# Swapping the token halves of odd heads in a convolution by band matmuls, and making all bands by one product

## The chip, the cores and the metric

One NeuronCore of a Trainium2 chip. The metric is the device time of one execution in microseconds (us). A profile's span is some 1.7 to 2.1 us shorter than the time of the same execution, so times are compared with times and spans with spans. In this kernel TensorE does the matrix products, into tiles that the program places in banks of a memory called PSUM; VectorE, ScalarE and GpSimd do the element-wise work. The granted clock is the share of full speed at which TensorE was allowed to run.

## The reference

`x` is (8, 4096, 192): batch, tokens, channels; 8 heads of 24 channels. Each head has 7 taps, made positive by a softmax. A causal convolution over tokens is followed by a two-layer block with h cos(h) in between.

```python
w = exp(weight - max) / (sum + 1e-9)                    # per head, 7 taps
out[b, s, head] = sum_k w[head, k] * x_pad[b, s + k, head]   # 6 zero tokens ahead
h = out.reshape(32768, 192) @ w_in                      # d_ff = 2048
g = h * cos(h)
result = g @ w_out                                      # 32768 x 192, fp32
```

## The kernel before

Tokens are worked on in units of 1024 (eight blocks of 128 tokens, one token per partition) and in steps of 512 tokens, 64 steps in all. A block is convolved by a matmul with a band matrix, which has the 7 taps of a head along its diagonal. It is cut in two row halves of 64 partitions (tokens), which are seen at work at the same time (the timeline in the prediction shows a matmul of each starting at 109.66 us). The program keeps them on different PSUM banks. Only the last 6 tokens of the block before matter, and these lie in the lower half. So a head needs three matmuls of 64 rows by 192 columns: upper half, lower half, lower half of the block before (`prev`).

```python
    E, KP = 32 + K - 1, 8
    mask = consts.tile([128, E, KP], BF16)          # 1 where a tap lies on the diagonal
    ...
    prod = consts.tile([128, H, E, KP], BF16)
    for hs in (slice(0, 4), slice(4, 8)):           # mask times taps, then a sum over taps
        nc.vector.tensor_tensor(out=prod[:, hs], in0=mask..., in1=wn[:, hs]..., op=ALU.mult)
        for m in (4, 2):
            nc.vector.tensor_tensor(out=prod[:, hs, :, 0:m], in0=prod[:, hs, :, 0:m], in1=prod[:, hs, :, m : 2 * m], op=ALU.add)
        for q in range(4):
            p = slice(32 * q, 32 * q + 32)
            nc.vector.tensor_tensor(out=band[p, hs, 32 * q : 32 * q + E], in0=prod[p, hs, :, 0], in1=prod[p, hs, :, 1], op=ALU.add)
    ...
    def cast_unit(u, n0=0, n1=UB):                  # fp32 tokens to bf16, on GpSimd
        copy = nc.scalar.copy if u == 0 and n0 == 0 else nc.gpsimd.tensor_copy
        ...
        copy(out=bf[u][:, n0 + 1 : n1 + 1, :].rearrange("p n (h k r) -> p (n h) k r", h=H, k=NC),
             in_=x_tiles[u][:, n0:n1, :].rearrange("p n (h r k) -> p (n h) k r", h=H, k=NC))
    ...
    def conv_part(u, c, n0=0, n1=UB):               # four heads, two halves at a time
        ps = h_pool.tile([128, 2, T], FP32, name="h")
        ...
        mm(0, up, start=True)                       # heads 0, 1: bank 0; heads 2, 3: bank 1
        mm(2, lo, start=True)
        m = mm(1, up)
        mm(2, lo, 1)                                # 1: the block before
        mm(3, lo)
        turn = Turn()                               # keeps the halves on different banks
        turn.mark(m, mm(3, lo, 1))
        yield
        turn.wait(mm(0, lo))
        mm(0, lo, 1)
        mm(1, lo)
        turn.wait(mm(2, up))
        mm(1, lo, 1, stop=True)
        mm(3, up, stop=True)
        yield
        ...                                         # ScalarE takes the result out of PSUM
```

The order of work in a step is written down: `h0` to `h7` are the eight tiles of h (6 matmuls of 64 rows by 512 columns each), `c1` and `c2` the first and the second six of the twelve matmuls of a conv part (four heads of a unit; there is one such part in a step), `m8` stands for 8 pairs (upper, lower) of the second layer's matmuls (o_ps, 64 rows by 192 columns). The h tiles and the conv share three PSUM buffers. ScalarE makes the cosine (`s`), VectorE multiplies it with h, and that frees the buffer. In `ACT_ORDER`, `P` and `Q` take results of o_ps out of PSUM, and `ec` those of the conv.

```python
    h_pool = ctx.enter_context(tc.tile_pool(name="h_ps", bufs=3, space=PSUM))
    PE_ORDER = "h0 c1 m8 c2 h1 m8 h2 h3 m16 | h4 h5 m8 h6 m12 h7 m12"
    ACT_ORDER = "P s0 ec s1 s2 s3 Q s4 s5 s6 s7"
```

Of the kernel before, what the change touches and what calls it, by code (L numbers as in the profile page):

```python
# [9 lines left out]
BF16 = mybir.dt.bfloat16  # L10
AF = mybir.ActivationFunctionType
ALU = mybir.AluOpType
# [4 lines left out]
def kernel(  # L17
# [8 lines left out]
    nc = tc.nc  # L26
    B, S, D = x.shape
    H, K = weight.shape
# [13 lines left out]
    NC = D // 64  # L42
    R = G // NC
# [3 lines left out]
    consts = ctx.enter_context(tc.tile_pool(name="consts", bufs=1))  # L47
# [16 lines left out]
    x_tiles = {}  # L64
# [13 lines left out]
    for q in range(2):  # L78
        for t in range(2):
            nc.sync.dma_start(out=w_f[64 * t : 64 * t + 64, :, q * HP : (q + 1) * HP, :].rearrange("p k j f -> p k (j f)"),  # L80
                              in_=w_src[t, :, :, q * HP * 128 : (q + 1) * HP * 128])
# [11 lines left out]
    def keep_warm(n):  # L93
        for _ in range(n):
# [11 lines left out]
    xb0 = xbf_pool.tile([128, UB + 1, D], BF16, name="x_bf")  # L106
    nc.gpsimd.memset(xb0[:, 0, :], 0.0)

    E, KP = 32 + K - 1, 8
    mask = consts.tile([128, E, KP], BF16)  # L110
    nc.gpsimd.memset(mask[0:32], 0.0)
    nc.gpsimd.affine_select(out=mask[0:32], in_=mask[0:32], compare_op=ALU.not_equal, fill=1.0, base=1 - K,
                            pattern=[[1, E], [1, KP]], channel_multiplier=-1)
    for q in range(1, 4):
        nc.gpsimd.tensor_copy(out=mask[32 * q : 32 * q + 32], in_=mask[0:32])
    ident = consts.tile([128, 128], BF16)
    nc.gpsimd.memset(ident, 0.0)
    nc.gpsimd.affine_select(out=ident, in_=ident, compare_op=ALU.not_equal, fill=1.0, base=0, pattern=[[1, 128]],
                            channel_multiplier=-1)
    wn = consts.tile([128, H, 1, KP], BF16)  # L120
    nc.vector.memset(wn, 0.0)
    band = consts.tile([128, H, 256], BF16)
    nc.vector.memset(band, 0.0)

# [2 lines left out]
    wexp = consts.tile([128, H, K], FP32)  # L127
# [4 lines left out]
    nc.vector.tensor_reduce(out=wsum[:, :, 0], in_=wexp, axis=mybir.AxisListType.X, op=ALU.add)  # L132
    winv = consts.tile([128, H, 1], FP32)
    nc.vector.reciprocal(winv, wsum)
    nc.vector.tensor_tensor(out=wn[:, :, 0, 0:K], in0=wexp, in1=winv.to_broadcast([128, H, K]), op=ALU.mult)


    prod = consts.tile([128, H, E, KP], BF16)
    for hs in (slice(0, 4), slice(4, 8)):
        nc.vector.tensor_tensor(out=prod[:, hs], in0=mask.rearrange("p (o e) k -> p o e k", o=1).to_broadcast([128, 4, E, KP]),  # L140
                                in1=wn[:, hs].to_broadcast([128, 4, E, KP]), op=ALU.mult)
        for m in (4, 2):
            nc.vector.tensor_tensor(out=prod[:, hs, :, 0:m], in0=prod[:, hs, :, 0:m], in1=prod[:, hs, :, m : 2 * m], op=ALU.add)  # L143
        for q in range(4):
            p = slice(32 * q, 32 * q + 32)
            nc.vector.tensor_tensor(out=band[p, hs, 32 * q : 32 * q + E], in0=prod[p, hs, :, 0], in1=prod[p, hs, :, 1], op=ALU.add)  # L146

    w = consts.tile([128, NC, NP, 128], BF16)
    wo = consts.tile([128, NP, 2, D], BF16)
# [18 lines left out]
    bf = {}  # L168

    def cast_unit(u, n0=0, n1=UB):  # L170
        copy = nc.scalar.copy if u == 0 and n0 == 0 else nc.gpsimd.tensor_copy
        if u == 0:
            bf[u] = xb0
        else:
            bf[u] = xbf_pool.tile([128, UB + 1, D], BF16, name="x_bf")
            if u % UPS == 0:
                nc.gpsimd.memset(bf[u][:, 0, :], 0.0)  # L177
            else:
                nc.gpsimd.tensor_copy(out=bf[u][:, 0, :], in_=bf[u - 1][:, UB, :])  # L179

        copy(out=bf[u][:, n0 + 1 : n1 + 1, :].rearrange("p n (h k r) -> p (n h) k r", h=H, k=NC),  # L181
             in_=x_tiles[u][:, n0:n1, :].rearrange("p n (h r k) -> p (n h) k r", h=H, k=NC))
        bf.pop(u - 2, None)

    ct_tiles = {}
# [1 line left out]
    def conv_view(ps, n):  # L187

        return ps[:, :, 0 : n * 2 * G].rearrange("p b (n k i r) -> p b i n k r", n=n, k=NC, i=2)

    def conv_mm(u, c, pv, i, rows, prev, n0, n1, **flags):
        h = 4 * c + i
        return nc.tensor.matmul(  # L193
            out=pv[:, i // 2, i % 2],
            lhsT=band[rows, h, 128 if prev else 0 : 256 if prev else 128],
            rhs=bf[u][rows, n0 + 1 - prev : n1 + 1 - prev, h * G : (h + 1) * G].rearrange("p n (k r) -> p n k r", k=NC),
            skip_group_check=True, **flags)

    def conv_out(u, c, ps, n0, n1, copies, double=False):
        for b in range(2):  # L200
            w0 = (2 * c + b) * 2 * R
            o = ct_tiles[u][:, n0:n1, :, :, w0 : w0 + 2 * R].rearrange("p n k t w -> p (n k) t w")
            i = ps[:, b, 0 : (n1 - n0) * 2 * G].rearrange("p (m t w) -> p m t w", t=1, w=2 * R)
            if double:
                copies[b](o, i.to_broadcast([128, (n1 - n0) * NC, 2, 2 * R]))  # L205
            else:
                copies[b](o[:, :, 0, :], i[:, :, 0, :])  # L207

    def conv_part(u, c, n0=0, n1=UB):


        ps = h_pool.tile([128, 2, T], FP32, name="h")
        pv = conv_view(ps, n1 - n0)
        up, lo = slice(0, 64), slice(64, 128)

        def mm(i, rows, prev=0, **flags):
            return conv_mm(u, c, pv, i, rows, prev, n0, n1, **{"start": False, "stop": False, **flags})

        mm(0, up, start=True)
        mm(2, lo, start=True)  # L220
        m = mm(1, up)
        mm(2, lo, 1)
        mm(3, lo)
        turn = Turn()
        turn.mark(m, mm(3, lo, 1))
        yield
        turn.wait(mm(0, lo))
        mm(0, lo, 1)
        mm(1, lo)
        turn.wait(mm(2, up))  # L230
        mm(1, lo, 1, stop=True)
        mm(3, up, stop=True)
        yield
        if c == 0 and u not in ct_tiles:
            ct_tiles[u] = ct_pool.tile([128, UB, NC, 2, 64], BF16, name="ct")
        conv_out(u, c, ps, n0, n1, [nc.scalar.copy] * 2)
        yield
# [14 lines left out]


    cast_unit(0, 0, NB)
    cast_unit(0, NB, UB)
    ct_tiles[0] = ct_pool.tile([128, UB, NC, 2, 64], BF16, name="ct")
    cT[0] = cT_pool.tile([128, UB, NC, 128], BF16, name="cT")
    copies = [nc.scalar.copy, nc.vector.tensor_copy]
# [35 lines left out]
    for q in range(2):  # L294
        for i in range(2):
            nc.sync.dma_start(out=wo_f[:, q * HP : (q + 1) * HP, i], in_=wo_src[:, q * HP : (q + 1) * HP, i])
    nc.gpsimd.tensor_copy(out=w[:, :, HP:NP], in_=w_f[:, :, HP:NP])
    cast_unit(1)
    for q in range(2):
        nc.gpsimd.tensor_copy(out=wo[:, q * HP : (q + 1) * HP], in_=wo_f[:, q * HP : (q + 1) * HP])  # L300
# [67 lines left out]
    for t in range(NT + 2):  # L368
        u, second = divmod(t, TPU)
        cu, cc = (u + 2, 0) if second else (u + 1, 1)  # L370
        conv = {"c": conv_part(cu, cc) if cu < NU else iter(())}
        if t == 0:
            conv["d"] = conv_part(1, 0)
        act, done, h, step = (ACT_ORDER if t > 1 else ACT_FIRST[t]).split(), set(), {}, 0
# [72 lines left out]
```

## Time and profile before

| | before |
|---|---|
| time, median | 745.55 us |
| span of the profile | 744.1 us |
| TensorE, VectorE, ScalarE, GpSimd busy | 98%, 83%, 84%, 18% |
| one step of 512 tokens in the steady part | 11.120 us |

The prediction below shows the lines of the page and of the timelines. In a timeline the columns are: start, busy time, engine, line of the kernel, operation, what it writes and reads, shapes, count, and in brackets the idle time ahead of it with what ended it. A matmul's bar (0.24 us with 192 columns) is longer than the time between two starts of one half (0.082 us), so bars overlap, and starts are what is read here.

### The profile page before, as it was taken

How to read it: one execution, taken by the hardware profiler on the slowest of the kernel's cores; microseconds unless marked ns; L12 is line 12 of the kernel's file. 1: busy time of each engine (PE TensorE's matmuls, PEld its weight loads, DVE VectorE, ACT ScalarE, POOL GpSimd, SP SyncE). 2: the span in 40 equal slices, each digit the busy share in tenths (PEclk: the TensorE clock that was granted, in tenths of full speed). 3: DMA queues.
4: the chain of work that ended last, by engine and by line, in shares of the span. 5: the costliest groups of instructions: out<-in, count | busy, mean ns of one | idle time of the engine just before them, and what ended most of it. 6: DMA issues, size and time to landing. Idle time of an engine off the chain costs nothing.

```text
span 744.1 us, 26716 instructions
## 1 busy us (share of the span) xinstructions
PE 727.9 (98%) x12073; PEld 647.4 (87%) x12073; DVE 619.7 (83%) x541; ACT 624.2 (84%) x776; POOL 134.2 (18%) x111
## 2 busy tenths in 40 slices
PE   5899999999999999999999999999999999999997
PEld 3489999999999999999999999999999999999876
DVE  7788888888888888888888888888888888888893
ACT  3788888888888888888888888888888888888883
POOL 4522102222102222201222201222201222201000
PEclk9999999999999999999999999999999999999999
DMA  7753354354355454354354255354245454243302
GB/s 171 181 118 95 100 129 104 92 130 100 95 129 110 86 129 104 91 129 120 75 129 111 87 127 126 73 126 119 83 122 129 78 119 124 81 118 86 87 23 65
DMA packets 167939, 79.96 MB, mean 107 GB/s; under 512 B 99474, under 2 KB 167058, under 8 KB 167826
## 3 DMA queue, kind: packets, MB, share of 16 engines
q1 hardware_dynamic: 167824, 78.26, 42.9%
q8 instruction: 94, 1.54, 0.9%
q14 instruction: 19, 0.16, 0.1%
q10 hardware_dynamic: 2, 0.00, 0.0%
HBM read 28.31 MB, written 25.17 MB: 72 GB/s over the span
## 4 chain that ended last, share of the span: by engine, by line
PE 96%; DVE 3%; ACT 1%; issue 0%; DVEq 0%
PE h L315 47%; PE o_ps L341 45%; PE h L193 3%; DVE g L325 1%; DVE band L146 0%; DVE prod L143 0%; ACT cs L321 0%; DVE prod L140 0%; ACT ct L207 0%; PE o_ps L95 0%; ACT o_sb L353 0%; DVE w L291 0%; PE h L274 0%; PE o_ps L102 0%; DVE zero L90 0%
## 5 line engine op out<-in xcount | busy, mean ns | idle before, releaser
L325 DVE TENSOR_TENSOR g<-h,cs 128x1024 bf16<-128x1024 f32 x512 | 605.3, 1221 | 107.4 <-ACT cs L321 100.5
L321 ACT ACTIVATE cs<-h 128x1024 bf16<-128x1024 f32 x512 | 511.5, 1025 | 75.0 <-PE h L315 70.2
L341 PE MATMUL o_ps<-wo,g 64*128 64x192 bf16 x8192 | 451.4, 243 | 1.2 <-ACT o_sb L353 1.2
L341 PEld LDWEIGHTS <-g 64*128 64x128 bf16 x8192 | 419.2, 94 | 35.5 <-SPq L159 1.8
L315 PE MATMUL h<-cT,w 64*128 64x512 bf16 x3072 | 436.4, 377 | 4.3 <-DVE g L325 2.0
L315 PEld LDWEIGHTS <-w 64*128 64x128 bf16 x3072 | 233.1, 94 | 40.3 <-issue 6.0
L243 POOL COPY ct<-ct 128x1536 bf16<-128x1536 bf16 (+1 forms) x32 | 46.4, 1449 | 548.0 <-ACT ct L207 542.5
L193 PE MATMUL h<-x_bf,band 64*128 64x192 bf16 (+1 forms) x776 | 73.0, 244 | 5.1 <-DVE band L146 4.7
L181 POOL CAST x_bf<-x_f 128x1536 bf16<-128x1536 f32 (+1 forms) x32 | 72.4, 2262 | 2.1 <-DMA x_f<-in_x_dram 2.1
L207 ACT CAST ct<-h 128x384 bf16<-128x384 f32 (+1 forms) x126 | 54.0, 480 | 21.3 <-PE h L193 21.3
L353 ACT COPY o_sb<-o_ps 128x384 f32<-128x384 f32 x128 | 61.3, 479 | 10.1 <-PE o_ps L341 8.2
L193 PEld LDWEIGHTS <-band 64*128 64x128 bf16 (+1 forms) x776 | 55.3, 95 | 11.2 <-DVE band L146 5.3
L179 POOL COPY x_bf<-x_bf 128x192 bf16<-128x192 bf16 x24 | 8.6, 358 | 0.0
L95 PE MATMUL o_ps<-zero 128*128 128x512 bf16 x19 | 6.3, 493 | 1.3 <-DVE zero L90 1.3
L205 ACT CAST ct<-h 128x384 bf16<-128x384 f32 x2 | 1.0, 480 | 6.9 <-PE h L193 6.9
L95 PEld LDWEIGHTS <-zero 128*128 128x128 bf16 x19 | 2.0, 116 | 4.3 <-issue 1.9
L300 POOL CAST wo<-wo_f 128x1536 bf16<-128x1536 f32 x2 | 2.9, 1469 | 4.2 <-DMA wo_f<-in_moe_w_out_dram 4.2
L146 DVE TENSOR_TENSOR band<-prod 32x152 bf16<-32x152 bf16 x8 | 3.3, 417 | 0.1
L143 DVE TENSOR_TENSOR prod<-prod 128x608 bf16<-128x608 bf16 (+1 forms) x4 | 3.0, 760 | 0.1
L98 ACT ACT_TABLE_LOAD x1 | 1.3, 1283 | 1.3 <-PEq L431 1.3
L205 DVE CAST ct<-h 128x384 bf16<-128x384 f32 x2 | 1.1, 558 | 0.9 <-ACT ct L205 0.8
L177 POOL MEMSET x_bf<- 128x192 bf16 x7 | 1.8, 258 | 0.0
(36 smaller groups left out, 20.9 us busy)
## 6 DMA issues: line engine op xcount, KB each, us to landing
out_dram<-o_sb SPq DMA_DIRECT2D x64, 384.0 KB, 3.0
x_f<-in_x_dram SPq DMA_DIRECT2D x31, 768.0 KB, 5.6
w_f<-in_moe_w_in_dram SPq DMA_DIRECT2D x4, 384.0 KB, 7.8
wo_f<-in_moe_w_out_dram SPq DMA_DIRECT2D x4, 384.0 KB, 5.0
x_f<-in_x_dram SPq DMA_DIRECT2D x2, 384.0 KB, 4.3
cT<-ct SPq DMA_TRANSPOSE x32, 5.6
w_row<-in_weight_dram ACTq DMA_DIRECT2D x1, 0.2 KB
```

Of the source, the lines that this page charges most:

```text
L95: nc.tensor.matmul(out=idle, lhsT=zero[:, 0:128], rhs=zero, start=True, stop=True)
L146: nc.vector.tensor_tensor(out=band[p, hs, 32 * q : 32 * q + E], in0=prod[p, hs, :, 0], in1=prod[p, hs, :, 1], op=ALU.add)
L179: nc.gpsimd.tensor_copy(out=bf[u][:, 0, :], in_=bf[u - 1][:, UB, :])
L181: copy(out=bf[u][:, n0 + 1 : n1 + 1, :].rearrange("p n (h k r) -> p (n h) k r", h=H, k=NC), in_=x_tiles[u][:, n0:n1, :].rearrange("p n (h ...
L193: return nc.tensor.matmul(out=pv[:, i // 2, i % 2], lhsT=band[rows, h, 128 if prev else 0 : 256 if prev else 128], rhs=bf[u][rows, n0 + 1 ...
L207: copies[b](o[:, :, 0, :], i[:, :, 0, :])
L243: nc.gpsimd.tensor_copy(out=ct[:, n0:n1, :, 1, :], in_=ct[:, n0:n1, :, 0, :])
L315: nc.tensor.matmul(out=h[:, i, :], lhsT=w[rows, k, j, :], rhs=c[rows, n0 : n0 + NB, k, :], start=(k == 0), stop=(k == NC - 1))
L321: nc.scalar.activation(out=cs, in_=h, func=AF.Sin, bias=math.pi / 2.0, scale=1.0)
L325: nc.vector.tensor_tensor(out=g_tiles[t][:, 2 * j : 2 * j + 2, :], in0=h, in1=cs, op=ALU.mult)
L341: m = nc.tensor.matmul(out=o_ps[tt, b][:, si * D : (si + 1) * D], lhsT=g_tiles[tt][rows, f, s * 128 : (s + 1) * 128], rhs=wo[rows, f // 2, ...
L353: nc.scalar.copy(o_sb[t][:, 2 * b : 2 * b + 2, :].rearrange("p s d -> p (s d)"), o_ps.pop((t, b))[:, 0 : 2 * D])
```

## The change

The intent: give both row halves the same work. If the tokens of the odd heads are stored with the two halves of each block exchanged, the odd heads' last 6 tokens lie in the upper half, and so does their third matmul. Four heads then need 6 and 6 matmuls in place of 4 and 8. The cast becomes three copies (even heads; odd heads down; odd heads up). The bands are made by one product over all heads, four sums, and eight copies dealt to VectorE, ScalarE and GpSimd.

```diff
-    prod = consts.tile([128, H, E, KP], BF16)
-    ... (mask times taps and sums by groups of four heads, as above)
+    prod = consts.tile([128, K, H, E], BF16)
+    nc.vector.tensor_tensor(out=prod, in0=mask.rearrange("p k (o e) -> p k o e", o=1).to_broadcast([128, K, H, E]),
+                            in1=wn.rearrange("p h (k o) -> p k h o", o=1).to_broadcast([128, K, H, E]), op=ALU.mult)
+    for d, n, m in ((0, 3, 3), (0, 1, 1), (2, 1, 4), (0, 1, 2)):
+        nc.vector.tensor_tensor(out=prod[:, d : d + n], in0=prod[:, d : d + n], in1=prod[:, d + m : d + m + n], op=ALU.add)
+    copies = [nc.vector.tensor_copy, nc.scalar.copy, nc.gpsimd.tensor_copy]
+    for odd in range(2):
         for q in range(4):
+            e0 = 32 * (q ^ (2 * odd))
+            copies[(4 * odd + q) % 3](out=band[32 * q : 32 * q + 32, odd:H:2, e0 : e0 + E],
+                                      in_=prod[32 * q : 32 * q + 32, 0, odd:H:2, :])
     ... (cut)
-        copy(out=bf[u][:, n0 + 1 : n1 + 1, :].rearrange("p n (h k r) -> p (n h) k r", h=H, k=NC),
-             in_=x_tiles[u][:, n0:n1, :].rearrange("p n (h r k) -> p (n h) k r", h=H, k=NC))
+        o = bf[u][:, n0 + 1 : n1 + 1, :].rearrange("p n (h t k r) -> t p (n h) k r", t=2, k=NC, r=R)
+        i = x_tiles[u][:, n0:n1, :].rearrange("p n (h t r k) -> t p (n h) k r", t=2, k=NC, r=R)
+        copy(out=o[0], in_=i[0])
+        copy(out=o[1, 0:64], in_=i[1, 64:128])
+        copy(out=o[1, 64:128], in_=i[1, 0:64])
     ... (cut)
+        mm(0, 0, start=True)      # head, half; 0 is the upper half
+        mm(2, 1, start=True)
+        mm(1, 0)
+        mm(2, 1, 1)
+        m = mm(1, 0, 1)
+        turn.mark(m, mm(3, 1))
         yield
+        m = mm(2, 0)
+        turn.wait(m, mm(0, 1))
+        mm(3, 0)
+        mm(0, 1, 1)
+        mm(3, 0, 1, stop=True)
+        mm(1, 1, stop=True)
```

More of the change, by code (lines that the diff above doesn't have):

```diff
@@ L107 @@
     nc.gpsimd.memset(xb0[:, 0, :], 0.0)
-    E, KP = 32 + K - 1, 8
-    mask = consts.tile([128, E, KP], BF16)
+    E = 32 + K - 1
+    mask = consts.tile([128, K, E], BF16)
     nc.gpsimd.memset(mask[0:32], 0.0)
     nc.gpsimd.affine_select(out=mask[0:32], in_=mask[0:32], compare_op=ALU.not_equal, fill=1.0, base=1 - K,
-                            pattern=[[1, E], [1, KP]], channel_multiplier=-1)
+                            pattern=[[1, K], [1, E]], channel_multiplier=-1)
     for q in range(1, 4):
@@ L119 @@
                             channel_multiplier=-1)
-    wn = consts.tile([128, H, 1, KP], BF16)
-    nc.vector.memset(wn, 0.0)
+    wn = consts.tile([128, H, K], BF16)
     band = consts.tile([128, H, 256], BF16)
@@ L134 @@
     nc.vector.reciprocal(winv, wsum)
-    nc.vector.tensor_tensor(out=wn[:, :, 0, 0:K], in0=wexp, in1=winv.to_broadcast([128, H, K]), op=ALU.mult)
-    prod = consts.tile([128, H, E, KP], BF16)
-    for hs in (slice(0, 4), slice(4, 8)):
-        nc.vector.tensor_tensor(out=prod[:, hs], in0=mask.rearrange("p (o e) k -> p o e k", o=1).to_broadcast([128, 4, E, KP]),
-                                in1=wn[:, hs].to_broadcast([128, 4, E, KP]), op=ALU.mult)
-        for m in (4, 2):
-            nc.vector.tensor_tensor(out=prod[:, hs, :, 0:m], in0=prod[:, hs, :, 0:m], in1=prod[:, hs, :, m : 2 * m], op=ALU.add)
+    nc.vector.tensor_tensor(out=wn, in0=wexp, in1=winv.to_broadcast([128, H, K]), op=ALU.mult)
+    prod = consts.tile([128, K, H, E], BF16)
[5 more added lines that the diff above has]
+    for odd in range(2):
         for q in range(4):
-            p = slice(32 * q, 32 * q + 32)
-            nc.vector.tensor_tensor(out=band[p, hs, 32 * q : 32 * q + E], in0=prod[p, hs, :, 0], in1=prod[p, hs, :, 1], op=ALU.add)
+            e0 = 32 * (q ^ (2 * odd))
+            copies[(4 * odd + q) % 3](out=band[32 * q : 32 * q + 32, odd:H:2, e0 : e0 + E],
+                                      in_=prod[32 * q : 32 * q + 32, 0, odd:H:2, :])
     w = consts.tile([128, NC, NP, 128], BF16)
@@ L213, in conv_part @@
         pv = conv_view(ps, n1 - n0)
-        up, lo = slice(0, 64), slice(64, 128)
+        sides = [slice(0, 64), slice(64, 128)]
         def mm(i, rows, prev=0, **flags):
-            return conv_mm(u, c, pv, i, rows, prev, n0, n1, **{"start": False, "stop": False, **flags})
-        mm(0, up, start=True)
-        mm(2, lo, start=True)
-        m = mm(1, up)
-        mm(2, lo, 1)
-        mm(3, lo)
+            return conv_mm(u, c, pv, i, sides[rows], prev, n0, n1, **{"start": False, "stop": False, **flags})
+        mm(0, 0, start=True)
[3 more added lines that the diff above has]
+        m = mm(1, 0, 1)
         turn = Turn()
-        turn.mark(m, mm(3, lo, 1))
+        turn.mark(m, mm(3, 1))
         yield
-        turn.wait(mm(0, lo))
-        mm(0, lo, 1)
-        mm(1, lo)
-        turn.wait(mm(2, up))
-        mm(1, lo, 1, stop=True)
-        mm(3, up, stop=True)
+        m = mm(2, 0)
[4 more added lines that the diff above has]
+        mm(1, 1, stop=True)
         yield
```

## The prediction

- The lower half's sums (11,119 and 10,954 ns) are made of the times between two starts of one half. The starts in the trace of the changed kernel give them: 82.5 ns with 192 columns (114 runs of 24 o_ps matmuls, 12 a half) and 215.8 ns with 512 (228 groups of six h matmuls, three a half), at a granted clock of 1.00. The kernel before shows that the halves run on independently: o_ps matmuls start at 109.66, 109.74 and 109.82 us, while conv matmuls that come ahead of them in the program start as late as 109.83 us. The trace does not name the half of a matmul, but the counts (of the first six conv matmuls, two above and four below) fit.
- The sum came to 5.6 us for the steady part and 1.3 us for the start, 6.9 us in all. The bands' product and sums both were to be done at about 9.0 us. The 9.9, 12.0 and 18.1 us follow from that 9.0, which was the author's estimate; no trace of the kernel before has the product's new form. For the sums alone, its trace gives an estimate of 1.7 us (a VectorE product of 1216 elements took 0.79 us and one of 56 took 0.22, so 912 elements would take 0.64 and 304 some 0.34).

> **What bounds the kernel now.** I read, in this order: the chain of waits, the costliest groups, the timeline of one steady stretch engine by engine, and the first 20 us.
>
> The chain and the three matmul groups of the page:
>
> ```profile
> PE 96%; DVE 3%; ACT 1%; issue 0%; DVEq 0%
> ...
> L341 PE MATMUL o_ps<-wo,g 64*128 64x192 bf16 x8192 | 451.4, 243 | 1.2 <-ACT o_sb L353 1.2
> L315 PE MATMUL h<-cT,w 64*128 64x512 bf16 x3072 | 436.4, 377 | 4.3 <-DVE g L325 2.0 <-ACT w L291 1.1 <-DVE w L291 0.8
> ...
> L193 PE MATMUL h<-x_bf,band 64*128 64x192 bf16 (+1 forms) x776 | 73.0, 244 | 5.1 <-DVE band L146 4.7
> ```
>
> TensorE is the bound, and nearly all matmuls use 64 rows: two row halves can work at once. So the question is which half. The chain in order of time gives the length of one step (one tile of 512 tokens); the same link comes back after 11.11 us (11.120 us on average from 45 to 689 us):
>
> ```profile
> 101.17 1.36 PE h L315 x12
> ...
> 112.28 1.36 PE h L315 x12
> ```
>
> The timeline of TensorE around the conv of such a step (start, length, group, count):
>
> ```profile
> 108.93 0.81 PE L315 MATMUL h<-cT,w 64*128 64x512 bf16 x5
> 109.49 0.33 PE L193 MATMUL h<-x_bf,band 64*128 64x192 bf16 x3
> 109.66 0.24 PE L341 MATMUL o_ps<-wo,g 64*128 64x192 bf16 x1
> 109.66 0.24 PE L193 MATMUL h<-x_bf,band 64*128 64x192 bf16 x1
> 109.74 0.24 PE L341 MATMUL o_ps<-wo,g 64*128 64x192 bf16 x1
> 109.74 0.24 PE L193 MATMUL h<-x_bf,band 64*128 64x192 bf16 x1
> ...
> 112.11 0.37 PE L315 MATMUL h<-cT,w 64*128 64x512 bf16 x1
> 112.12 0.24 PE L341 MATMUL o_ps<-wo,g 64*128 64x192 bf16 x1
> 112.21 1.46 PE L315 MATMUL h<-cT,w 64*128 64x512 bf16 x11
> ```
>
> At 109.66 the upper half has run out of conv work (2 matmuls) and starts on o_ps, while the lower half still does conv (4 matmuls). The halves are thus two queues that run on independently, each starting a 192-column matmul every 0.082 us. The lower one has more to do: per step 24 matmuls of h, 64 of o_ps and 8 of conv, against 24, 64 and 4 above.
>
> [...] for the lower half 24 x 215.8 + 72 x 82.5 = 11,119 ns, against the 11.120 us measured. So **the lower row half is busy all the time, and it is the bound**; the upper one idles 4 x 82.5 = 330 ns a step. [...] the same two additions took 1.89 us while a GpSimd cast ran (6.22 to 7.44) and 1.22 us later. [...]
>
> **The change, part by part.**
>
> Conv in the steady state. A head needs three matmuls: upper rows, lower rows, and lower rows of the block before. With the halves of odd heads swapped, their third one goes to the upper half. Per part of 4 heads: 6 and 6 in place of 4 and 8; the number of matmuls, 12, stays, and no weight load is added. The lower half then has 70 short matmuls: 24 x 215.8 + 70 x 82.5 = 10,954 ns, so 165 ns less. There are 62 parts; two fall in step 0, one in step 1, and 59 in full steps. Ceiling: 59 x 0.165 = 9.7 us.
>
> The wait behind it. h tiles live in three buffers; the third h of a step reuses the first one's. That path, from the timelines of ScalarE and VectorE:
>
> ```profile
> 109.78 1.02 ACT L321 ACTIVATE cs<-h 128x1024 bf16<-128x1024 f32 x1 [0.17 <-PE h L315]
> ...
> 110.83 1.23 DVE L325 TENSOR_TENSOR g<-h,cs 128x1024 bf16<-128x1024 f32 x1 [0.41 <-ACT cs L321]
> ```
>
> The first h ends at 109.74 (108.93 + 0.81), cosine to 110.80, product to 112.06, and the upper half starts the third h at 112.11. That start is already set by VectorE; the lower half comes at 112.21 and does not feel it. Between the first and the third h stand all 8 lower conv matmuls, so after the change the lower half would be there at 112.21 - 0.165 = 112.04, and the buffer comes free at 112.11 as before: both engines were idle ahead of those two instructions, so this path does not shrink. A **new wait of 0.07 us** a step; the saving is 0.165 - 0.07 = 0.095 us, and 59 x 0.095 = **5.6 us**. I looked for the next such wait: the sixth h waits for the third's product; as everything after the third h moves along with it, I find some 0.08 us of room there.
>
> Casts on GpSimd. A unit's cast (1536 elements, 2.30 us) becomes three of 768; one of 768 took 1.22 us on 128 partitions, and I take 64 partitions to cost the same. So 3.66 us, 31 times, in a step of 11 us in which GpSimd is otherwise idle after 4.1 us; the result is read a step later. It is hidden. Products of VectorE took 1.225 us beside GpSimd work and 1.221 without, so the longer overlap costs it nothing to speak of.
>
> The start. The bands of heads 4 to 7 come last:
>
> ```profile
> 5.03 0.79 DVE L140 TENSOR_TENSOR prod<-mask,wn 128x1216 bf16<-128x1216 bf16 x1
> 5.85 1.89 DVE L143 TENSOR_TENSOR prod<-prod 128x608 bf16<-128x608 bf16 x2
> 7.77 1.71 DVE L146 TENSOR_TENSOR band<-prod 32x152 bf16<-32x152 bf16 x4
> ...
> 11.60 1.70 DVE L146 TENSOR_TENSOR band<-prod 32x152 bf16<-32x152 bf16 x4
> ```
>
> and TensorE waits from 10.05 to 13.36 for them. [...] Eight copies are dealt to three engines, three on ScalarE at some 0.3 us each: 9.9. But ScalarE's cast of the first half unit, done by 6.83 before, now stands behind these copies, as three of 384 elements, which I put at 0.7 each (1.23 for 768): about 12.0. All 32 conv matmuls follow, in place of 24 after 13.36. The granted clock from 13.3 to 17.0 us was 0.63 on average; eight took 0.64 us there and 0.34 at full clock. The rest of the way to the steady h stream (15.34 to 18.85) stays at 3.5 us. So h starts at 12.0 + 2.6 + 3.5 = 18.1, or about 17 at full clock, against 18.85: 0.7 to 1.9 us earlier, I take **1.3 us**. Steps 0 and 1 are bound by ScalarE and VectorE, and pass it on.
>
> Sum: 5.6 + 1.3 = 6.9 us; 745.5 - 6.9 = **738.6 us**, 0.9% less.
>
> **Rivals.** (a) Nothing takes the lower half's place: the full 9.7 us, 734.5 us with the start. For it speaks that the lower half is full to within 1 ns; against it the third h, whose start is already VectorE's. (b) VectorE or ScalarE becomes the bound: they are busy 83% and 84%, and back to back their instructions start every 1.14 and 0.92 us, 8 x 1.14 = 9.1 us a step. As a rate neither binds; as a latency VectorE does, once a step. Should several h buffers do so, 0.05 us a step are left: 741 us. (c) The slack was hidden anyway, as the upper half runs ahead on o_ps: then no gain. Against it: running ahead helps the upper half alone; the lower starts without a gap. (d) The start gets worse, because the casts on ScalarE and GpSimd now queue behind the band copies: up to 2 us lost[...]; 741 us.
>
> **Range and chances.** The steady part is worth 0.06 to 0.165 us a step (3.5 to 9.7 us), the start -1 to +2.5 us. The extremes hardly meet, so 734.5 to 741.5 us holds it 8 times in 10. 2% faster would be 730.6 us, below even the ceiling: 3%. Slower by 2% would need the bound to move: 2%.
>
> **What would show it.** The step should be 11.02 us in the chain, with conv matmuls in pairs, 6 a half; 10.95 says (a), 11.12 says (c). Idle time of TensorE ahead of the third h, ended by VectorE's product, should be about 0.07 us a step, where there was none. GpSimd should be busy near 175 us. [...] the first conv matmul should come near 12 us and the h stream near 18 us. I am wrong if swapped partitions make the GpSimd casts several times slower, or if TensorE's clock falls at the start.

## The result, and the profile after

The changed kernel took 740.13 us (739.96 to 740.39, 4 runs) against 745.53 us (745.43 to 746.20, 4 runs). The ratio is 0.9926, with a 95% interval of 0.9909 to 0.9943. A ratio here is the mean time of one kernel's runs over the mean of the other's in the same rounds, so it isn't quite the ratio of the medians. The gain is 5.4 us, 0.7%; 6.9 us were predicted, and the time lies in the range. All changes in this document are under 2%, so they rest on such intervals and on the lengths of the steps.

Three stretches add up to the 5.84 us between the two spans (744.07 and 738.23). To measure them I took the start of VectorE's first product of steps 2 and 60.

| | before | after | gain |
|---|---|---|---|
| up to step 2 | 44.11 us | 43.02 us | 1.09 us |
| 58 steps, 2 to 60 | 644.96 us, 11.120 each | 640.41 us, 11.042 each | 4.55 us |
| after that | 55.00 us | 54.79 us | 0.20 us |

The first row is not a clean measure. Between 5 and 25 us the mean granted clock was 0.83 in the profile before and 0.91 in the one after. The first three experiments leave everything up to step 2 as it was, so their profiles show the same two starts again. At 0.83, step 2 came at 44.11 us (before) against 43.45 and 43.53 (experiments one and two); at 0.91, at 43.71 (experiment three) against 43.02 (after). So at a like clock the new start gains 0.6 to 0.7 us, as far as these five profiles go. With 59 steps of 0.078 us and 0.1 us at the end (0.20 without step 60, which is one of the 59) that makes 5.3 to 5.4 us, as the times have it.

TensorE's groups on the page of the changed kernel (busy us and mean ns; then the idle time ahead):

```profile
L347 PE MATMUL o_ps<-wo,g 64*128 64x192 bf16 x8192 | 409.0, 243 | 1.2 <-ACT o_sb L359 1.2
L321 PE MATMUL h<-cT,w 64*128 64x512 bf16 x3072 | 402.9, 377 | 4.1 <-DVE g L331 1.7
...
L198 PE MATMUL h<-x_bf,band 64*128 64x192 bf16 (+1 forms) x776 | 55.3, 241 | 4.1 <-ACT x_bf L185 1.7
```

The counts and the length of one matmul are as before, but the busy times fell by 42, 34 and 18 us against the lines in the prediction. That is no saving of 94 us: a group's busy time is the union of its bars, and now the halves run the same groups side by side, their starts 0.02 us apart, so bars of the same group lie over each other. The page can't tell what the change is worth. TensorE is still busy 98% of the span. The weight loads are counted in the same way: 12,073 of them, of 94 ns in the median, covered 87% of the span before and 75% after, though their lengths add up to 1,138 us in both.

The timeline of TensorE in the steady part of the changed kernel:

```profile
107.35 0.83 PE L321 MATMUL h<-cT,w 64*128 64x512 bf16 x6
107.99 0.43 PE L198 MATMUL h<-x_bf,band 64*128 64x192 bf16 x6
108.24 0.84 PE L347 MATMUL o_ps<-wo,g 64*128 64x192 bf16 x16
108.90 0.43 PE L198 MATMUL h<-x_bf,band 64*128 64x192 bf16 x6
109.15 0.83 PE L321 MATMUL h<-cT,w 64*128 64x512 bf16 x6
109.80 0.84 PE L347 MATMUL o_ps<-wo,g 64*128 64x192 bf16 x16
110.55 1.47 PE L321 MATMUL h<-cT,w 64*128 64x512 bf16 x12
```

The conv no longer mixes with o_ps; 6 conv matmuls take 0.25 us from start to start (107.99 to 108.24), three pairs of 0.0825. But the last link shows the new wait. Eight pairs of o_ps begin at 109.80, so the third h could begin at 109.80 + 8 x 0.0825 = 110.46. It begins at 110.55. VectorE's product of the first h, in the timeline of VectorE, ends at 109.27 + 1.23 = 110.50, just ahead of it:

```profile
109.27 1.23 DVE L331 TENSOR_TENSOR g<-h,cs 128x1024 bf16<-128x1024 f32 x1 [0.41 <-ACT cs L327]
```

The chain in order of time shows the same as a length. The third and fourth h together take 1.38 us, the fifth and sixth 1.29 us with the same 12 matmuls:

```profile
102.30 1.29 PE h L321 x12
...
110.64 1.38 PE h L321 x12
```

No view lists that wait as idle time. A matmul's bar lasts 0.24 us, and a hold-up of 0.09 us between starts disappears under it.

The start, in the timelines of VectorE, ScalarE and TensorE of the changed kernel:

```profile
5.02 2.38 DVE L137 TENSOR_TENSOR prod<-mask,wn 128x2128 bf16<-128x2128 bf16 x1
7.43 1.56 DVE L140 TENSOR_TENSOR prod<-prod 128x912 bf16<-128x912 bf16 x4
...
9.02 0.98 ACT L147 COPY band<-prod 32x152 bf16<-32x152 bf16 x3 [3.33 <-DVE prod L140]
10.03 0.70 ACT L185 CAST x_bf<-x_f 128x384 bf16<-128x384 f32 x1
...
12.22 1.09 PE L198 MATMUL h<-x_bf,band 128*128 128x96 bf16 x22 [1.19 <-ACT x_bf L187]
13.79 0.50 PE L198 MATMUL h<-x_bf,band 128*128 128x96 bf16 x8 [0.48 <-DVE ct L210]
...
17.68 4.24 PE L321 MATMUL h<-cT,w 64*128 64x512 bf16 x22 [1.04 <-DVE w L297]
```

The product took 2.38 us. ScalarE's cast stands behind its band copies, and the conv waits for the last piece of it. The last eight conv matmuls wait once more, for VectorE to take earlier results out of PSUM.

### The profile page after: what moved, and what is told of

It is laid out like the page before. It is cut to its first block, busy times and chain, and to the rows that moved or that the text cites. A ratio compares the mean times of both kernels' runs of the same rounds, so it can differ in the third digit from the quotient of the medians.

```text
span 738.2 us, 26755 instructions
## 1 busy us (share of the span) xinstructions
PE 723.3 (98%) x12073; PEld 553.9 (75%) x12073; DVE 620.2 (84%) x534; ACT 626.8 (85%) x781; POOL 177.7 (24%) x177
## 4 chain that ended last, share of the span: by engine, by line
PE 94%; ACT 0%; issue 0%; SPq 0%
PE o_ps L347 46%; PE h L321 44%; PE h L198 4%; ACT o_sb L359 0%; SPq L161 0%
## 5 line engine op out<-in xcount | busy, mean ns | idle before, releaser
L347 PEld LDWEIGHTS <-g 64*128 64x128 bf16 x8192 | 362.1, 94 | 67.4 <-SPq L161 1.8
L347 PE MATMUL o_ps<-wo,g 64*128 64x192 bf16 x8192 | 409.0, 243 | 1.2 <-ACT o_sb L359 1.2
L321 PE MATMUL h<-cT,w 64*128 64x512 bf16 x3072 | 402.9, 377 | 4.1 <-DVE g L331 1.7
L321 PEld LDWEIGHTS <-w 64*128 64x128 bf16 x3072 | 166.1, 94 | 89.0 <-issue 6.4
L198 PE MATMUL h<-x_bf,band 64*128 64x192 bf16 (+1 forms) x776 | 55.3, 241 | 4.1 <-ACT x_bf L185 1.7
L198 PEld LDWEIGHTS <-band 64*128 64x128 bf16 (+1 forms) x776 | 38.0, 94 | 17.6 <-issue 3.2
L186 POOL CAST x_bf<-x_f 64x768 bf16<-64x768 f32 (+1 forms) x32 | 38.7, 1208 | 2.0
L187 POOL CAST x_bf<-x_f 64x768 bf16<-64x768 f32 (+1 forms) x32 | 38.5, 1204 | 1.9
L185 POOL CAST x_bf<-x_f 128x768 bf16<-128x768 f32 (+1 forms) x32 | 38.9, 1217 | 0.1
L137 DVE TENSOR_TENSOR prod<-mask,wn 128x2128 bf16<-128x2128 bf16 x1 | 2.4, 2376 | 0.1
```

What stands on the lines that cost most here:

```text
L185: copy(out=o[0], in_=i[0])
L186: copy(out=o[1, 0:64], in_=i[1, 64:128])
L187: copy(out=o[1, 64:128], in_=i[1, 0:64])
L198: return nc.tensor.matmul(out=pv[:, i // 2, i % 2], lhsT=band[rows, h, 128 if prev else 0 : 256 if prev else 128], rhs=bf[u][rows, n0 + 1 ...
L321: nc.tensor.matmul(out=h[:, i, :], lhsT=w[rows, k, j, :], rhs=c[rows, n0 : n0 + NB, k, :], start=(k == 0), stop=(k == NC - 1))
L347: m = nc.tensor.matmul(out=o_ps[tt, b][:, si * D : (si + 1) * D], lhsT=g_tiles[tt][rows, f, s * 128 : (s + 1) * 128], rhs=wo[rows, f // 2, ...
```

## The experiments

Each one was timed against the kernel before in the same rounds (745.6 us in the set of the first four, 746.0 us in that of the last four, on another chip), and all give right results but the fourth. The changed kernel was timed in a third set (740.13 us, with 745.53 before), so a time set against it is good to some 0.5 us; the steps are the sharper measure. Lengths of a step are measured as in the table above.

### One pair of o_ps more ahead of the third h

```diff
-    PE_ORDER = "h0 c1 m8 c2 h1 m8 h2 h3 m16 | h4 h5 m8 h6 m12 h7 m12"
+    PE_ORDER = "h0 c1 m8 c2 h1 m9 h2 h3 m15 | h4 h5 m8 h6 m12 h7 m12"
```

> The changed kernel with one o_ps pair more ahead of the third h (9 in place of 8; 15 in place of 16 after the fourth). Theory: the step is held up 0.08 to 0.09 us by the wait of the third h for the first h's product, so one pair (0.0825 us) put into that wait makes it vanish: step 10.95 to 10.97 us in place of 11.04, 4 to 5 us less than the changed kernel, some 735.5 us. Rival (the lower half's work is simply dearer than reckoned, or weight loads bound): the same matmuls are run, the step stays at 11.04, 740 us.

Measured: 736.40 us, ratio 0.9872 (0.9856 to 0.9889); step 10.972 us. The timeline of TensorE:

```profile
109.81 0.92 PE L347 MATMUL o_ps<-wo,g 64*128 64x192 bf16 x18
110.56 1.47 PE L321 MATMUL h<-cT,w 64*128 64x512 bf16 x12
```

Nine pairs from 109.81 end at 110.55, and the third h follows without a gap, as late as in the changed kernel though one pair more has been done. Nothing was removed, only one pair was moved, and the step became 0.070 us shorter. So the wait is real, and moving one pair gives back 0.070 us of it. Without it the balance gives 11.120 - 10.972 = 0.148 us of the 0.165; with it, it gave 0.078.

### Two pairs more

The same with `m10` and `m14`.

> The changed kernel with two pairs more ahead of the third h (10, and 14 after the fourth). Theory: the sixth h waits for the third's product, with some 0.08 us of room; two pairs use 0.165 us of it, so a second wait of about 0.08 us comes up at the sixth h: step about 11.04 us, 740 us, as without any move. Rival (the order of the pairs matters only for the third h): step 10.95 us as with one pair.

Measured: 741.23 us, ratio 0.9936; step 11.052 us. The timeline of TensorE, third and fourth h, then fifth and sixth:

```profile
111.20 1.48 PE L321 MATMUL h<-cT,w 64*128 64x512 bf16 x12
...
113.65 1.57 PE L321 MATMUL h<-cT,w 64*128 64x512 bf16 x12
```

and VectorE's product of the third h:

```profile
113.12 1.22 DVE L331 TENSOR_TENSOR g<-h,cs 128x1024 bf16<-128x1024 f32 x1
```

Now it is the second group of 12 that is longer by 0.09 us. The sixth h is its second half. In the instruction starts it begins at 114.40 us, 0.054 us after the product that ends at 114.346; in the changed kernel the held-up third h too begins 0.054 us after the product that frees its buffer, and in this run that wait is gone. So the sixth h waits for the third's buffer. In the changed kernel it began 0.117 us after that product, so it had 0.117 - 0.054 = 0.063 us to spare: one pair (0.0825 us) is already a little over it, the second one wholly. The move is a balance between two waits, and of no pair, one and two that were tried, one is best.

### One pair more, in the kernel before

The same edit as in the first experiment (`m9`, `m15`), in the kernel before.

> The kernel before with the same move of one pair. Theory: there the lower half is busy throughout and the third h's wait is hidden, so nothing is gained: step 11.12 us, 745.5 us (within 0.5). Rival (the move is good for any kernel, the wait was there before too): some 0.08 us a step, 741 us.

Measured: 746.38 us, ratio 1.0010 (0.9995 to 1.0025); step 11.134 us. Nothing gained; the step is even 0.014 us longer, and the time is 0.8 us above that of the kernel before in the same rounds (within 0.5 us was expected; the interval includes no change). So the wait cost the kernel before nothing. It became one through the change.

### No conv matmuls for the block before (wrong results on purpose)

In the changed kernel, in every conv part but those of the first unit, which has a conv of its own.

```diff
         mm(2, 1, start=True)
-        mm(1, 0)
-        mm(2, 1, 1)
-        m = mm(1, 0, 1)
+        m = mm(1, 0)
         ...
-        mm(3, 0)
-        mm(0, 1, 1)
-        mm(3, 0, 1, stop=True)
+        mm(3, 0, stop=True)
         mm(1, 1, stop=True)
```

> The changed kernel without the matmuls for the block before in the steady state (wrong results on purpose): 4 and 4 in place of 6 and 6 conv matmuls. Theory: the path first h, cosine, product, third h is 2.75 us long whatever TensorE does in it; it already sets the step, so taking 0.165 us of matmuls out of it gains nothing or little: step 11.02 to 11.04, 739.5 to 740 us. Rival (TensorE's rows bound): step 10.88 us, 9.5 us less, 730.5 us.

Measured: 740.14 us, ratio 0.9923; step 11.040 us. Taking out a third of the conv's matmuls gains nothing over the changed kernel (740.13 us, 11.042). The timeline of TensorE, from the first h to the third:

```profile
107.48 0.83 PE L317 MATMUL h<-cT,w 64*128 64x512 bf16 x6
...
109.76 0.84 PE L343 MATMUL o_ps<-wo,g 64*128 64x192 bf16 x16
110.68 0.61 PE L317 MATMUL h<-cT,w 64*128 64x512 bf16 x4
```

The o_ps pairs are done at 109.76 + 0.66 = 110.42, and the third h comes 0.26 us later. The first h ended at 107.48 + 0.83 = 108.31; from there to the third h it is 2.37 us. In the changed kernel it is 110.55 - 108.18 = 2.37, and in the kernel before 112.11 - 109.74 = 2.37. This path (cosine, product and the hand-overs between them) keeps its length in all three. (The 2.75 us of the expectation are the same path, counted from the start of the first h's last matmul: 107.80 to 110.55 in the changed kernel.)

### The new bands alone

The kernel before with the new product, sums and copies; no halves swapped (`e0 = 32 * q`), casts in one operation.

> The kernel before with the new making of the bands alone, no halves swapped, casts in one operation. Theory: the steady step stays 11.12 us, and only the start gains: bands ready at 10 us, the cast of the first half unit on ScalarE in one operation done near 11.3, so conv starts a microsecond earlier than in the changed kernel and the h stream 1 to 2 us earlier than before: 743.5 to 744.5 us. Rival (the start gives nothing at the end, as steps 0 and 1 wait for loads of weights): 745.5 us.

Measured: 744.27 us, ratio 0.9977 (0.9963 to 0.9992); step 11.120 us, step 2 at 42.68 us in place of 44.11. The clock between 5 and 25 us was 0.83 in both. So the bands are worth 1.4 us (profile) to 1.7 us (times) and leave the steps alone. With the cast in one operation the conv begins earlier than in the changed kernel (12.22, after two matmuls at 10.79), as the timeline of TensorE shows:

```profile
11.30 1.20 PE L195 MATMUL h<-x_bf,band 128*128 128x96 bf16 x24 [2.94 <-ACT x_bf L183]
```

### The casts in three alone

The kernel before with the three copies of the change, but each half to itself (`o[1, 0:64]` from `i[1, 0:64]`).

> The kernel before with each cast split in three as in the change, without the swap. Theory: GpSimd's casts of the steady state are hidden: step 11.12 us, GpSimd busy some 43 us more; at the start ScalarE's cast comes ahead of the bands, so nothing shifts there: 745.5 us within 0.7. Rival (the longer GpSimd work slows VectorE's products [...]): products over 1.23 us, step longer than 11.12.

Measured: 746.23 us, ratio 1.0001 (0.9985 to 1.0018); step 11.120 us; VectorE's products took 1.221 us on average, as before. On the page GpSimd's share went from 18% to 24%:

```profile
L183 POOL CAST x_bf<-x_f 128x768 bf16<-128x768 f32 (+1 forms) x32 | 39.0, 1219 | 2.4 <-DMA x_f<-in_x_dram 2.4
L185 POOL CAST x_bf<-x_f 64x768 bf16<-64x768 f32 (+1 forms) x32 | 38.9, 1215 | 1.9
```

The third copy took as long. The 42 us more on GpSimd (176.5 against 134.2) cost the steady part nothing. Its start was 0.7 us later in the profile (step 2 at 44.81), but there the clock was lower too (0.74 between 5 and 25 us, against 0.83), and the times show no difference.

### An earlier cast

The changed kernel with ScalarE's cast of the first half unit issued ahead of the band copies.

```diff
+    cast_unit(0, 0, NB)
     for odd in range(2):
         for q in range(4):
             ... (the eight band copies)
-    cast_unit(0, 0, NB)
     cast_unit(0, NB, UB)
```

> The changed kernel with the first cast (ScalarE, first half unit) and all band copies exchanged in order, so that ScalarE casts while VectorE makes the product. Theory: the first conv matmuls start near 10.1 in place of 12.2 us (two at 10.8), the second half follows near 12.1 when GpSimd's casts end, so the h stream comes some 1.4 us earlier; step unchanged at 11.04: 738.7 us. Rival (VectorE's evacuations or the weights' cast set the start): under 0.5 us, 740 us.

Measured: 738.55 us, ratio 0.9901; step 11.042 us, step 2 at 41.09 us in place of 43.02. The timelines of ScalarE and TensorE:

```profile
5.60 0.69 ACT L178 CAST x_bf<-x_f 128x384 bf16<-128x384 f32 x1
...
10.11 0.84 PE L191 MATMUL h<-x_bf,band 128*128 128x96 bf16 x16 [0.23 <-ACT band L258]
12.08 0.76 PE L191 MATMUL h<-x_bf,band 128*128 128x96 bf16 x14 [1.14 <-POOL x_bf L180]
```

ScalarE casts while VectorE is still at the product, the first half's conv is done two microseconds earlier, and the second half waits for GpSimd's cast, as expected. The profile's 1.9 us are more than the 1.6 us of the times; in this one execution the clock stayed full at the start (1.00 between 5 and 25 us, against 0.91 in the changed kernel's profile). So the earlier cast is worth some 1.6 us, with the doubt of two sets.

### Both together

> The changed kernel with one pair more ahead of the third h and the earlier cast at the start. Theory: the two gains add up, as one is in the steady steps and the other before them: 4 to 5 us and 1.4 us, some 734 us. If the start's gain is swallowed, 735.5 us.

Measured: 734.93 us (733.21 to 735.55), ratio 0.9848 (0.9834 to 0.9863); step 10.974 us. The gains of the order and of the start (3.7 and 1.6 us by the medians) add up to within a few tenths: 740.1 - 734.9 = 5.2 us. All four runs of this kernel are faster than all runs of either one alone.

## Why the prediction was right

**The bound.** That the lower half sets the pace was right. Once the halves were even and the wait was out of the way, the step came to 10.972 us, against a floor of 10.954 reckoned from the starts of 82.5 and 215.8 ns.

**The new wait.** It was foreseen, at the right place and with the right cause, and the first, third and fourth experiments show it. It is one of two terms of the sum that were mis-sized: 0.07 us was put down, and 11.042 - 10.954 = 0.088 was measured. In the instruction starts the lower half's first matmul of the third h came 0.077 us later than its queue allowed, and the next one after 0.227 in place of 0.216 us. I had worked out only when the third h may begin. In the starts both halves then begin 0.006 us apart (110.547 and 110.553 us) and are 0.018 us apart at the next matmul, near their usual 0.02; that makes the rest. So a step gained 0.078 us, not 0.095, and 59 x 0.078 = 4.6 us in place of 5.6.

**The room ahead of the sixth h.** Put at 0.08 us, and 0.063 by the starts in the changed kernel. With one pair moved, the lower half's starts (mean of 30 steps) show hold-ups of 0.003 us at the third h and 0.014 at the sixth. Their sum, 0.017 us, accounts for what lies between 10.972 and the floor of 10.954.

**The casts** are hidden, as predicted: in the steady part one of 64 partitions that crosses to the other half took 1.22 us and one of 128 in place took 1.23 (in the sixth experiment one of 64 in place took 1.22), and GpSimd is busy 178 us (175 were said). The 1.225 us given for products beside GpSimd work are not what the trace shows: it is 1.222 us beside it and 1.221 without, so the conclusion is the firmer.

**The start.** This is the other mis-sized term: 1.3 us were put down, and 0.6 to 0.7 measured at a like clock. That the two profiles show 1.09 us looks like luck of the clock. The single terms: product 2.38 us and sums 1.56, both done at 9.0 (9.0 predicted), the last ScalarE cast done at 12.2 (12.0). The product ran at half the rate of the sums: sums of 912 and 304 elements took 0.632 and 0.314 us, which makes 0.52 ns an element and a fixed 0.16 us; less the same fixed part, an element of the product (2128 in 2.376 us) took 1.04 ns. The product of the kernel before, in another layout, took 0.792 us for 1216 elements, which with that fixed part is 0.52 ns each as well. What in the new form halves the rate was not shown. The h stream was reckoned at 18.1 us, or 17 at full clock, and 1.3 us lay between. At a clock of 0.83 it came at 18.20 (experiments one and two, against 18.85 before), so the first figure was right. In the changed kernel's profile the clock was full up to 17.98 us, and the h stream still came only at 17.68: the 32 conv matmuls did not run in one go, the last eight waited until 13.79 us for VectorE. Rival (d), that casts behind the band copies eat up gain, was right in kind: the bands alone win 1.4 us in the profile where the whole change wins 0.6 to 0.7, and the seventh experiment wins some 1.6 us by turning the order round.

**What would show it.** One line was wrong: the wait was to be seen as idle time of TensorE. No view shows it so; it has to be read from starts.

**The other rivals.** (a) is ruled out by the step of 11.042 us in place of 10.954, and (c) because it is below 11.120. (b) is true as a latency, at one buffer; at a second one only after the move of two pairs.

**Still open:** the 0.1 us gained after step 60 was not traced, and the start was never timed with the clock held the same.

## What to carry to other kernels

When the starts show two halves of an engine as two queues, add up each one's work. Here the fuller one was the bound (11.119 us reckoned, 11.120 measured), and the even split, half the difference or 0.165 us a step, gave 0.148 once the wait was out of the way. Before counting on all of that, look for the waits that stand just behind the bound, in particular the path that gives a buffer back: here it was 0.1 us short of showing, and took half of the gain (0.088 of 0.165 us a step). Moving work into such a wait was a cheap way to remove it: one pair gave back 0.070 us a step here, but two brought the step to 11.052 us again, as the next buffer had only 0.063 us of room. And compare two starts only at a like granted clock: here some 0.4 of 1.1 us seem to have come from it.
